# Layer norm's constant as a third entry of the statistics, and a rearranged last token tile, in a Conformer block

## The chip, the cores and the metric

One core of one Trainium2 chip. The metric is the device time of the program in microseconds (us). A profile's span is some 4 us shorter than that time; stages are compared by their place in the span.

Engines: PE is TensorE (matmuls), DVE VectorE, ACT ScalarE, POOL GpSimd, SP SyncE, which issues most transfers.

## The reference, cut to what matters

A Conformer block on tokens `x` of 2 x 4000 x 512 in bf16: feed forward, attention, convolution, feed forward, with a layer norm before each and one at the end.

```python
def _layernorm(x, axis=-1, eps=1e-05):
    m = jnp.mean(x, axis=axis, keepdims=True)
    v = jnp.var(x, axis=axis, keepdims=True)
    return (x - m) / jnp.sqrt(v + eps)
...
h = _layernorm(x3)
h = _silu(h @ w_ff2_a) @ w_ff2_b
x4 = x3 + 0.5 * h
return _layernorm(x4)
```

## The kernel before

Tokens are worked in tiles of 127, four tiles to a chunk. A layer norm is: statistics (`bn_stats`, six values a tile), aggregate (`bn_aggr`, mean and variance), variance plus epsilon, that to the power -1/2 on POOL, normalise. In the head of the kernel and in its last tile each step waits for the one before.

```python
def ln_mean(self, sl, ti):
    self.S.op("DVE", lambda e: e.bn_aggr(self.mv[sl][:, ti, :], self.st[sl][:, ti, :]),
              reads=[self.b_st[sl][ti]], writes=[self.b_mv[sl][ti]])
def ln_factor(self, sl, ti):
    S.op("DVE", lambda e: e.tensor_scalar(self.va[sl][:, ti:ti + 1], self.mv[sl][:, ti, 1:2], EPS, None, ALU.add),
         reads=[self.b_mv[sl][ti]], writes=[self.b_va[sl][ti]])
    S.op("POOL", lambda e: e.tensor_tensor(out=self.rs[sl][:, ti:ti + 1], in0=self.va[sl][:, ti:ti + 1],
                                           in1=self.neghalf[0:TILE, ti:ti + 1], op=ALU.pow),
         reads=[self.b_va[sl][ti], self.b_neghalf], writes=[self.b_rs[sl][ti]])
# ... (ln_aggr does the same for four tiles at once)

def ff_last(self, c, old):                # the last chunk of the kernel
    # ... first matmuls of the feed forward, all 16 blocks
    for ti in range(token_tiles(c)):
        for f in range(FC):                                     # 16 matmuls of 512 columns
            self.ff_second(f, ti, *blocks[f], f == FC - 1)
        self.residual(self.Yb[ti][0:TILE, :], self.b_Y[ti], c * TPC + ti, 0.5)   # XT = XT + 0.5 * Y, on DVE
        self.ln_stats(c, sl, ti)
        self.ln_mean(sl, ti)
        self.ln_factor(sl, ti)
        self.ln_norm(c, sl, ti, self.osb[0][:, ti, :], self.b_osb[0][ti], "DVE")
        self.store_out(c, self.osb[0], self.b_osb[0], ti, ti + 1, ("SP", "ACT"))
```

Waits are placed by a helper. Before each instruction it emits a `wait_ge` for every semaphore value that the engine is not yet known to have seen.

```python
for key in sorted(req, key=str):
    ev = req[key]
    if clk.get(key, 0) >= ev.val:      # this engine has waited for it before
        continue
    if key == e and e in self.NOSELF:  # NOSELF = ("PE",)
        ...
    self.eng[e].wait_ge(self.sem[ev.key], ev.val)
```

## Time and profile before

| what | before |
|---|---|
| time, median of three runs | 2047.35 us (2047.34 to 2047.93) |
| span in the profile | 2043.1 us |
| PE busy | 99% of the span |
| first statistics to PE's fifth block (head) | 7.52 us (3.60 to 11.12) |
| PE's end to the end of the last normalise (tail) | 2.94 us (2037.28 to 2040.22) |
| the last store, from issue to landing | 2.6 us on SP's queue, 2.1 on ACT's |

How to read it: PE runs back to back nearly everywhere, so a step of another engine counts only where PE stands idle for it, and after PE's end. This is the chain of waits of the kernel before in the head (start, length, what; `issue` is time in which the engine waits for nothing that the profile shows):

```profile
4.32 0.19 DVE work L719
4.52 0.02 issue
4.54 0.17 DVE work L724
4.71 0.07 issue
4.78 0.56 POOL work L726
5.34 0.02 issue
5.37 0.16 DVE work L672
5.52 0.10 DVE work L719
```

Each tile goes round aggregate (L719), plus-constant (L724), power (L726), shift (L672), and the next tile's aggregate follows. And this is the kernel before in the transfers' view at the store of the last tile; q14 and q8 are queues that the profile labels "instruction" (packets, MB, share of 16 engines); the last number of an issue is us to landing:

```profile
q14 instruction: 3, 0.02, 2.2%
q10 hardware_dynamic: 30, 0.02, 2.0%
...
out_dram<-work SPq DMA_DIRECT2D x1, 112.0 KB, 2.6
out_dram<-work ACTq DMA_DIRECT2D x1, 15.0 KB, 2.1
```

### The profile page before, as it was taken

Reading aid. Unit: us, or ns where it says so; the run is one execution under the profiler, and the core shown is the slowest. Engines: PE = TensorE matmul, PEld = TensorE weight load, DVE = VectorE, ACT = ScalarE, POOL = GpSimd, SP = SyncE. Lnnn points to the kernel's source line nnn. Section 1 sums busy time; section 2 is a strip of 40 time slices with the busy share of each in tenths; the row PEclk is TensorE's granted clock in tenths of the full one; section 3 lists DMA queues with packets and bytes.
Section 4 is the critical chain, followed back from the end, with each engine's and each line's share of the span. In section 5 each row is a group of like instructions: output and inputs, shape, how many; then the busy total and the mean of one; then the engine's idle time right before and its main releaser. Section 6 shows DMA issues by size and latency. Waiting matters only on the chain.

```text
span 2043.1 us, 24518 instructions
## 1 busy us (share of the span) xinstructions
PE 2029.6 (99%) x9649; PEld 1028.9 (50%) x9649; DVE 1093.0 (54%) x2264; ACT 743.9 (36%) x1274; POOL 109.4 (5%) x236
## 2 busy tenths in 40 slices
PE   9999999999999999999999999999999999999998
PEld 5555555554444444445444444444445555555555
DVE  4244443334556667666766676667674444434434
ACT  3433333333333333333333333333345443443433
POOL 1000000000000000000000000000011000000000
PEclk9999999999999999999999999999999999999999
DMA  8222245320101111114421111111143111111111
GB/s 185 52 62 62 53 101 124 96 70 8 26 16 29 24 31 26 29 24 96 106 55 23 28 29 29 24 28 29 39 135 93 32 31 42 32 31 41 28 35 38
DMA packets 253121, 104.42 MB, mean 51 GB/s; under 512 B 193412, under 2 KB 252487, under 8 KB 252999
## 3 DMA queue, kind: packets, MB, share of 16 engines
q1 hardware_dynamic: 252751, 102.61, 21.1%
q8 instruction: 78, 1.28, 0.3%
q14 instruction: 44, 0.36, 0.1%
q10 hardware_dynamic: 248, 0.18, 0.0%
HBM read 33.77 MB, written 23.34 MB: 28 GB/s over the span
## 4 chain that ended last, share of the span: by engine, by line
PE 97%; DVE 1%; issue 0%; POOL 0%; DMA 0%; ACT 0%; POOLq 0%; SPq 0%; DVEq 0%; ACTq 0%
PE s L500 55%; PE y L500 42%; DVE work L612 0%; DVE wff L1177 0%; POOL work L726 0%; ACT work L550 0%; DVE xt L753 0%; DMA work<-work 0%; DMA xt<-in_x_dram 0%; DVE work L634 0%; POOL work L1186 0%; DVE work L547 0%; DVE wff L1071 0%; DVE work L920 0%; DVE work L719 0%
## 5 line engine op out<-in xcount | busy, mean ns | idle before, releaser
L550 ACT ACTIVATE work<-s 128x508 bf16<-128x508 f32 (+3 forms) x1060 | 621.7, 587 | 1212.8 <-PE s L500 1208.3
L500 PE MATMUL s<-work,wff 128*128 128x508 bf16 (+5 forms) x2624 | 628.2, 371 | 2.3 <-DVE work L547 1.8
L500 PE MATMUL s<-work,keys 128*128 128x508 bf16 (+1 forms) x2048 | 516.7, 374 | 0.1
L500 PE MATMUL y<-work,keys 128*128 128x508 bf16 (+2 forms) x2048 | 504.3, 373 | 0.4 <-DVE work L1000 0.4
L500 PE MATMUL y<-wff,work 128*127 128x512 bf16 x1992 | 501.2, 379 | 0.0
L920 DVE TENSOR_TENSOR work<-work 128x508 f32<-128x508 f32 (+2 forms) x496 | 334.6, 675 | 279.9 <-ACT work L550 278.8
L500 PEld LDWEIGHTS s<-work,wff 128*128 128x128 bf16 x2624 | 252.2, 98 | 278.6 <-issue 6.2
L500 PEld LDWEIGHTS y<-wff,work 128*127 128x127 bf16 x1992 | 273.7, 137 | 171.4
L500 PEld LDWEIGHTS s<-work,keys 128*128 128x128 bf16 x2048 | 199.5, 98 | 231.9 <-issue 0.6
L500 PEld LDWEIGHTS y<-work,keys 128*128 128x128 bf16 (+1 forms) x2048 | 193.5, 97 | 234.0 <-issue 6.2
L753 DVE SCALAR_TENSOR_TENSOR xt<-y,xt 127x512 bf16<-127x512 f32 x126 | 78.5, 683 | 360.1 <-PE y L500 360.1
L612 DVE BATCH_NORM_STATS2 work<-xt 127x6 f32<-127x512 bf16 x312 | 197.3, 680 | 6.3 <-DMA xt<-in_x_dram 6.2
L500 PE MATMUL s<-work 128*127 128x512 bf16 (+3 forms) x776 | 197.0, 378 | 2.2 <-DVE work L1293 1.2
L621 POOL TENSOR_TENSOR work<-work 127x4 f32<-127x4 f32 (+1 forms) x76 | 76.5, 1007 | 1133.0 <-DVE work L619 1133.0
L500 PEld LDWEIGHTS s<-work 128*127 128x127 bf16 (+1 forms) x776 | 94.9, 124 | 76.9 <-issue 3.7
L634 DVE TENSOR_SCALAR work<-xt,work 127x512 bf16<-127x512 bf16 x307 | 110.8, 407 | 26.2 <-POOL work L621 22.9
L753 DVE SCALAR_TENSOR_TENSOR xt<-s,xt 127x512 bf16<-127x512 f32 x55 | 38.0, 692 | 144.6 <-PE s L500 144.6
L753 DVE SCALAR_TENSOR_TENSOR xt<-s,work,xt 127x512 bf16<-127x512 f32 x64 | 48.0, 751 | 32.1 <-PE s L500 31.5
L1075 DVE SCALAR_TENSOR_TENSOR wff<-wff,s 128x508 bf16<-128x508 f32 (+1 forms) x57 | 38.7, 679 | 41.6 <-PE s L500 41.4
L550 ACT ACTIVATE wff<-s 128x508 f32<-128x508 f32 (+1 forms) x67 | 39.5, 591 | 55.1 <-PE s L500 55.1
L550 ACT ACTIVATE work<-keys,work 128x508 bf16<-128x508 bf16 (+1 forms) x68 | 52.3, 775 | 1.4 <-DVE work L1191 1.3
L1156 POOL COPY wff<-wff 128x1 bf16<-128x1 bf16 x56 | 10.4, 187 | 635.3 <-DVE wff L1075 632.8
(83 smaller groups left out, 424.5 us busy)
## 6 DMA issues: line engine op xcount, KB each, us to landing
keys<-keysd SPq DMA_DIRECT2D x62, 128.0 KB, 2.3
keysd<-work SPq DMA_DIRECT2D x14, 448.0 KB, 3.2
out_dram<-work SPq DMA_DIRECT2D x14, 448.0 KB, 3.2
dcvd<-wff SPq DMA_DIRECT2D x48, 127.0 KB, 1.7
keys<-dcvd SPq DMA_DIRECT2D x12, 508.0 KB, 4.9
xt<-in_x_dram SPq DMA_DIRECT2D x13, 448.0 KB, 4.8
wff<-in_w_ff_a_dram SPq DMA_DIRECT2D x16, 256.0 KB, 5.4
work<-work SPq DMA_TRANSPOSE x208, 2.5
```

The lines of the kernel that those rows point to most:

```text
L500: self.S.op("PE", lambda e: e.matmul(out, lhsT, rhs, start=start, stop=stop, **kw), reads=reads, writes=[bank], inc=stop if inc is None el ...
L550: return self.S.op("ACT", lambda e: e.activation(out, in_, func, **kw), reads=reads, writes=writes)
L612: self.S.op("DVE", lambda e: e.bn_stats(self.st[sl][:, ti, :], x), reads=[b_x], writes=[self.b_st[sl][ti]])
L621: S.op("POOL", lambda e: e.tensor_tensor(out=self.rs[sl][:, 0:n], in0=self.va[sl][:, 0:n], in1=self.neghalf[0:TILE, 0:n], op=ALU.pow), rea ...
L634: self.S.op("DVE", lambda e: e.tensor_scalar(out, x, self.mv[sl][:, ti, 0:1], self.rs[sl][:, ti:ti + 1], ALU.subtract, ALU.mult), reads=[b ...
L753: self.S.op("DVE", lambda e: e.scalar_tensor_tensor(out=self.XT[g][rows], in0=ps[rows], scalar=scalar, in1=self.XT[g][rows], op0=ALU.mult, ...
L920: S.op("DVE", lambda e, p=p, n=n, acc=acc: e.tensor_tensor(out=acc, in0=acc, in1=self.P[p][0:n, 0:W], op=ALU.add), reads=[self.b_P[p], sel ...
L1075: self.S.op("DVE", lambda e: e.scalar_tensor_tensor(out=out, in0=th, scalar=1.0, in1=ps[:, 0:W], op0=ALU.add, op1=ALU.mult), reads=[b_ps, ...
L1156: S.op("POOL", lambda e: e.tensor_copy(self.G[gs][:, jj, 0:1], self.G[gp][:, jj, CHUNK:CHUNK + 1]), reads=[self.b_G[gp][jj]], writes=[self ...
```

## The change

First intent: no separate plus-constant. `bn_stats` leaves two entries of three values for a tile. Each tile's statistics get a third entry, set once, of 0, 0 and `D * EPS`, which adds to the sum of squares and to nothing else; the aggregate over nine values instead of six then yields variance plus epsilon by itself.

Second intent, the last tile only: the residual becomes a matmul with twice the identity, so PSUM holds 2·x3 + h, twice x4 (the layer norm does not mind the factor, if epsilon is taken four times: two from the third entries of the two halves, two from the square root's bias); the tile is made in two halves of 256 columns in two PSUM banks, so that the statistics of the first lie beside PE's second; the power on POOL becomes a square root on ACT and a reciprocal on DVE; and DVE and ACT normalise a half each.

```diff
-        self.st = [small(TPC * 6, ...)]
+        self.st = [small(TPC * 9, ...)]
...
 def ln_factor(self, sl, ti):
-        S.op("DVE", lambda e: e.tensor_scalar(self.va..., self.mv[sl][:, ti, 1:2], EPS, None, ALU.add), ...)
-        S.op("POOL", lambda e: e.tensor_tensor(out=self.rs..., in0=self.va[sl][:, ti:ti + 1], ...pow))
+        S.op("POOL", lambda e: e.tensor_tensor(out=self.rs..., in0=self.mv[sl][:, ti, 1:2], ...pow))
...     # the same in ln_aggr
 def ff_last(self, c, old):
+        S.op("DVE", lambda e: e.tensor_scalar(self.two, self.ident, 2.0, None, ALU.mult), ...)
...
+        self.act(self.nr1, self.onef, AF.Sqrt, [self.b_onef], [self.b_nr1])      # loads the table early
-        for ti in range(token_tiles(c)):
+        for ti in range(n - 1):
...
+        halves = [(self.Yb[k], self.b_Y[k], slice(m * D // 2, (m + 1) * D // 2)) for m, k in enumerate((0, ti))]
+        for m, (ps, b_ps, d) in enumerate(halves):
+            self.mm(ps[0:TILE, d], self.two[0:TILE, 0:TILE], self.XT[g][:, d], True, False, ...)
+            for f, (p, b_p) in enumerate(blocks):
+                self.mm(ps[0:TILE, d], p[:, ti * TILE:(ti + 1) * TILE], self.Wb[:, f, d], False, f == FC - 1, ...)
+            S.op("DVE", ... e.bn_stats(st[:, m, 0:6], ps[0:TILE, d]))
+        S.op("DVE", ... e.bn_aggr(self.mv[sl][:, ti, :], st.rearrange("p t s -> p (t s)")))   # 18 values
+        self.act(sd, self.mv[sl][:, ti, 1:2], AF.Sqrt, ..., bias=self.eps2[0:TILE])
+        S.op("DVE", ... e.reciprocal(self.rs[sl][:, ti:ti + 1], sd))
+        S.op("DVE", ... e.scalar_tensor_tensor(out=sh, in0=mean, scalar=-1.0, in1=rs, ...))  # shift
+            # half 0: DVE tensor_scalar (x - mean) * rs;  half 1: ACT Identity, scale=rs, bias=sh
+        self.store_out(c, self.osb[0], b_o, ti, ti + 2, ("SP", "ACT"))
...
 def constants(self):
+        for sl in range(self.LN_SLOTS):
+            S.op("DVE", ... e.memset(self.st[sl][:, :, 6:8], 0.0))
+            S.op("DVE", ... e.memset(self.st[sl][:, :, 8:9], D * EPS))
+        S.op("POOL", ... e.memset(self.eps2, 2 * EPS))
```

More of the change, by code (lines that the diff above doesn't have):

```diff
@@ L384, in memory @@
         self.b_late = [A.buf("late", k * 1024, 2 * CHUNK) for k in range(FC - self.NP)]
+        self.two = A.view(60 * 1024, 128)
+        self.b_two = A.buf("two", 60 * 1024, 256)
         ns = self.LN_SLOTS
@@ L396, in memory @@
         self.b_neghalf = Buf("neghalf")
-        self.st = [small(TPC * 6, parts=TILE).rearrange("p (t s) -> p t s", t=TPC) for _ in range(ns)]
+        self.st = [small(TPC * 9, parts=TILE).rearrange("p (t s) -> p t s", t=TPC) for _ in range(ns)]
         self.b_st = [[Buf("st") for _ in range(TPC)] for _ in range(ns)]
@@ L400, in memory @@
         self.b_mv = [[Buf("mv") for _ in range(TPC)] for _ in range(ns)]
-        self.va = [small(TPC, parts=TILE) for _ in range(ns)]
-        self.b_va = [[Buf("va") for _ in range(TPC)] for _ in range(ns)]
         self.rs = [small(TPC, parts=TILE) for _ in range(ns)]
@@ L412, in memory @@
         self.b_nr1 = Buf("nr1")
+        self.eps2 = small(1)
+        self.b_eps2 = Buf("eps2")
         self.onef = small(1)
@@ L611, in ln_stats @@
         x, b_x = self.tokens(c, ti, src)
-        self.S.op("DVE", lambda e: e.bn_stats(self.st[sl][:, ti, :], x), reads=[b_x], writes=[self.b_st[sl][ti]])
+        self.S.op("DVE", lambda e: e.bn_stats(self.st[sl][:, ti, 0:6], x), reads=[b_x], writes=[self.b_st[sl][ti]])
     def ln_aggr(self, sl, n, shift=False):
@@ L618, in ln_aggr @@
                  reads=[self.b_st[sl][ti]], writes=[self.b_mv[sl][ti]])
-        S.op("DVE", lambda e: e.tensor_scalar(self.va[sl][:, 0:n], self.mv[sl][:, 0:n, 1], EPS, None, ALU.add),
-             reads=self.b_mv[sl], writes=self.b_va[sl])
-        S.op("POOL", lambda e: e.tensor_tensor(out=self.rs[sl][:, 0:n], in0=self.va[sl][:, 0:n],
+        S.op("POOL", lambda e: e.tensor_tensor(out=self.rs[sl][:, 0:n], in0=self.mv[sl][:, 0:n, 1],
                                                in1=self.neghalf[0:TILE, 0:n], op=ALU.pow),
-             reads=self.b_va[sl] + [self.b_neghalf], writes=self.b_rs[sl])
+             reads=self.b_mv[sl] + [self.b_neghalf], writes=self.b_rs[sl])
         if shift:
@@ L723, in ln_factor @@
         S = self.S
-        S.op("DVE", lambda e: e.tensor_scalar(self.va[sl][:, ti:ti + 1], self.mv[sl][:, ti, 1:2], EPS, None, ALU.add),
-             reads=[self.b_mv[sl][ti]], writes=[self.b_va[sl][ti]])
-        S.op("POOL", lambda e: e.tensor_tensor(out=self.rs[sl][:, ti:ti + 1], in0=self.va[sl][:, ti:ti + 1],
+        S.op("POOL", lambda e: e.tensor_tensor(out=self.rs[sl][:, ti:ti + 1], in0=self.mv[sl][:, ti, 1:2],
                                                in1=self.neghalf[0:TILE, ti:ti + 1], op=ALU.pow),
-             reads=[self.b_va[sl][ti], self.b_neghalf], writes=[self.b_rs[sl][ti]])
+             reads=[self.b_mv[sl][ti], self.b_neghalf], writes=[self.b_rs[sl][ti]])
     def store_keys(self, c):
@@ L795, in ff_last @@
         S, late = self.S, FC - self.NP
+        S.op("DVE", lambda e: e.tensor_scalar(self.two, self.ident, 2.0, None, ALU.mult), reads=[self.b_ident], writes=[self.b_two])
         blocks = []
@@ L807, in ff_last @@
             self.tick()
-        sl = self.nxt("ln", self.LN_SLOTS)
-        for ti in range(token_tiles(c)):
+        self.act(self.nr1, self.onef, AF.Sqrt, [self.b_onef], [self.b_nr1])
+        sl, n = self.nxt("ln", self.LN_SLOTS), token_tiles(c)
+        for ti in range(n - 1):
             for f in range(FC):
@@ L817, in ff_last @@
             self.store_out(c, self.osb[0], self.b_osb[0], ti, ti + 1, ("SP", "ACT"))
+        ti, g = n - 1, c * TPC + n - 1
+        st, b_st = self.st[sl][:, ti:ti + 2, :], self.b_st[sl][ti:ti + 2]
+        halves = [(self.Yb[k], self.b_Y[k], slice(m * D // 2, (m + 1) * D // 2)) for m, k in enumerate((0, ti))]
+        for m, (ps, b_ps, d) in enumerate(halves):
+            self.mm(ps[0:TILE, d], self.two[0:TILE, 0:TILE], self.XT[g][:, d], True, False, [self.b_two, self.bx[g]], b_ps)
+            for f, (p, b_p) in enumerate(blocks):
+                self.mm(ps[0:TILE, d], p[:, ti * TILE:(ti + 1) * TILE], self.Wb[:, f, d], False, f == FC - 1,
+                        [self.b_Wb[f], b_p], b_ps)
+            S.op("DVE", lambda e, m=m, ps=ps, d=d: e.bn_stats(st[:, m, 0:6], ps[0:TILE, d]), reads=[b_ps], writes=[b_st[m]])
+        S.op("DVE", lambda e: e.bn_aggr(self.mv[sl][:, ti, :], st.rearrange("p t s -> p (t s)")),
+             reads=b_st, writes=[self.b_mv[sl][ti]])
+        sd, b_sd = self.sh[sl][:, ti:ti + 1], self.b_sh[sl][ti]
+        self.act(sd, self.mv[sl][:, ti, 1:2], AF.Sqrt, [self.b_mv[sl][ti], self.b_eps2], [b_sd], bias=self.eps2[0:TILE])
+        S.op("DVE", lambda e: e.reciprocal(self.rs[sl][:, ti:ti + 1], sd), reads=[b_sd], writes=[self.b_rs[sl][ti]])
+        o, b_o = self.osb[0][:, ti, :], self.b_osb[0]
+        mean, rs, sh = self.mv[sl][:, ti, 0:1], self.rs[sl][:, ti:ti + 1], self.sh[sl][:, ti:ti + 1]
+        b_mv, b_rs, b_sh = self.b_mv[sl][ti], self.b_rs[sl][ti], self.b_sh[sl][ti]
+        S.op("DVE", lambda e: e.scalar_tensor_tensor(out=sh, in0=mean, scalar=-1.0, in1=rs, op0=ALU.mult, op1=ALU.mult),
+             reads=[b_mv, b_rs], writes=[b_sh])
+        for m, (ps, b_ps, d) in enumerate(halves):
+            if m == 0:
+                S.op("DVE", lambda e, ps=ps, d=d: e.tensor_scalar(o[:, d], ps[0:TILE, d], mean, rs, ALU.subtract, ALU.mult),
+                     reads=[b_ps, b_mv, b_rs], writes=[b_o[ti]])
+            else:
+                self.act(o[:, d], ps[0:TILE, d], AF.Identity, [b_ps, b_sh, b_rs], [b_o[ti + 1]], bias=sh, scale=rs)
+        self.store_out(c, self.osb[0], b_o, ti, ti + 2, ("SP", "ACT"))
     def store_out(self, c, o, b_o, lo, hi, engs=("SP",)):
@@ L1293, in constants @@
         S.op("DVE", lambda e: e.memset(self.zero, 0.0), writes=[self.b_zero])
+        for sl in range(self.LN_SLOTS):
+            S.op("DVE", lambda e, sl=sl: e.memset(self.st[sl][:, :, 6:8], 0.0), writes=self.b_st[sl])
+            S.op("DVE", lambda e, sl=sl: e.memset(self.st[sl][:, :, 8:9], D * EPS), writes=self.b_st[sl])
         S.op("POOL", lambda e: e.memset(self.hl, 0.0), writes=self.b_hl)
@@ L1297, in constants @@
         S.op("POOL", lambda e: e.memset(self.onef, 1.0), writes=[self.b_onef])
+        S.op("POOL", lambda e: e.memset(self.eps2, 2 * EPS), writes=[self.b_eps2])
         S.op("DVE", lambda e: e.memset(self.XT[SHARED][HALF - 32:HALF], 0.0), writes=[self.bx[SHARED]])
```

## The prediction

> **What bounds the kernel now.** I read the page first (busy shares, the slices, the chain that ended last), then the waits, then the timeline and the chain of waits in the few stretches where TensorE is not the one that is busy.
>
> ```profile
> span 2043.1 us, 24518 instructions
> PE 2029.6 (99%) x9649; PEld 1028.9 (50%) x9649; DVE 1093.0 (54%) x2264; ACT 743.9 (36%) x1274; POOL 109.4 (5%) x236
> ...
> PE 97%; DVE 1%; issue 0%; POOL 0%; DMA 0%; ACT 0%; POOLq 0%; SPq 0%; DVEq 0%; ACTq 0%
> ...
> L619 DVE TENSOR_SCALAR work<-work 127x4 f32<-127x4 f32 x73 | 12.6, 172 | 2.5
> ```
>
> TensorE (PE) works for 99% of the span and is 97% of the chain that ended last. So of the first part of the change, which takes away one small VectorE (DVE) instruction per layer norm (the group L619 above, and L724 of 15 instructions at 146 ns), almost everything lies beside PE: 12.6 + 2.2 = 14.8 us of DVE work go, but DVE is busy 54% of the time and nobody waits for it. What can move the end are the places where PE stands still and a layer norm is the cause: the head, the last transposes before the convolution, the two chains around 1520 and 1547 us, and the tail. The tail, in the timeline:
>
> ```profile
> 2033.66 1.89 PE L500 MATMUL y<-wff,keys 128*127 128x512 bf16 x8
> ...
> 2035.39 1.89 PE L500 MATMUL y<-wff,work 128*127 128x512 bf16 x8
> ...
> 2036.37 0.41 DVE L634 TENSOR_SCALAR work<-xt,work 127x512 bf16<-127x512 bf16 x1 [0.67 <-POOL work L726]
> 2037.32 0.69 DVE L753 SCALAR_TENSOR_TENSOR xt<-y,xt 127x512 bf16<-127x512 f32 x1 [0.54 <-PE y L500]
> 2038.04 0.69 DVE L612 BATCH_NORM_STATS2 work<-xt 127x6 f32<-127x512 bf16 x1
> 2038.77 0.18 DVE L719 BATCH_NORM_AGGREGATE work<-work 127x2 f32<-127x6 f32 x1
> 2038.99 0.15 DVE L724 TENSOR_SCALAR work<-work 127x1 f32<-127x1 f32 x1
> 2039.22 0.55 POOL L726 TENSOR_TENSOR work<-work 127x1 f32<-127x1 f32 x1 [2.89 <-DVE work L724]
> 2039.81 0.41 DVE L634 TENSOR_SCALAR work<-xt,work 127x512 bf16<-127x512 bf16 x1 [0.66 <-POOL work L726]
> ```
>
> The reader is to see a strictly serial chain: PE ends at 2037.27 (residual's start less a hop of 0.05), then residual, statistics, aggregate, plus-constant, power, normalise, each 0.03 to 0.08 after the one before, until 2040.22. From there to the span's end at 2043.1 are 2.9 us of store (its issue at 2040.29, landing 2.6 us later), which the change leaves as it is: the same two pieces on the same two queues. The part that can shrink is 2.95 us, 0.14% of the kernel.
>
> **What the Trainium skill says.** (1) "TensorE: Matmul & The Clock Gate", Back-to-back issue gap: N/2.4 + 2.5 ns, 262 cycles for 256 columns, so about 109 ns. The trace has 254 columns at 107 ns in the head (20 matmuls, of which 16 with 254 columns, in 2.77 us) and 512 columns at 216 ns (8 in 1.89 us, the last one's own 379 ns counted). It agrees. (2) The same page, Weight-path perf modes: fast weight load needs a full 128-column weight. The tail's weights have 127 columns, and their load row says 137 ns against 98 ns for 128 columns, so they are slower, as stated. This matters, because the halves give each load only 107 ns of matmul to hide behind. (3) "ScalarE: Activation LUTs", What ACT_TABLE_LOAD costs: a table load of 1283 ns (the trace: 1283 exactly, four times) and a fixed cost plus 93 ns per pointer operand of an ACTIVATE (the trace: 604 ns for 127x512 out of PSUM without pointers, 766 with two; agrees within 25 ns). Its next section says that cheap functions such as identity are in every set; the trace has four loads in all, with copies and identities among silu, exp and sigmoid, so the final identity after the square root should bring no load of its own. (4) "PSUM — Partial Sum Buffer", PSUM bank collisions: two engines may not use one bank at a time. The change puts the halves in two banks, so DVE can read the first while PE writes the second. No run yet shows what would happen otherwise.
>
> **The tail, step by step.** Removed after PE's end: residual 0.69, plus-constant 0.15, power 0.55, and half of the statistics; the residual becomes a matmul with twice the identity, and the statistics of half one run while PE makes half two.
> PE: before 16 x 0.216 = 3.45 us, now 2 x 17 = 34 matmuls of 256 columns, 34 x 0.1077 = 3.66. PE ends 0.2 later.
> Half one's PE ends 1.83 after the tile begins (2033.83), at 2035.7. Its statistics wait in DVE's order behind tile 1's normalise (until 2036.78, now 0.2 earlier as tile 1 loses its plus-constant: 2036.6), run to about 2037.0 and are done before PE's end at 2037.47. Hidden.
> Statistics of half two out of PSUM: 674 ns for 512 columns in f32, and 690 against 620 ns for 508 and 444 columns, so 1.09 ns a column; 256 fewer give about 0.41, hop 0.05.
> Aggregate of 18 values: 179 ns for 6, 223 for 15, 250 for 21: about 0.235, hop 0.04.
> Square root on ScalarE (ACT): 202 ns for 128x1, a bias pointer on top: 0.25, hop 0.04.
> Reciprocal: 183 ns for 127x4, so 0.16, hop 0.04. Shift: 0.16 (as L672 in the head), hop 0.04.
> Normalise: ACT's half is last, as it alone needs the shift: 766 - 256 x 0.83 = 0.55, hop 0.04. (0.83 from the page's 593 ns for 508 and 490 ns for 381 columns.) DVE's half, out of PSUM where 512 columns took 806 ns and not 414, is some 0.5 from 0.1 after the shift's start and ends first.
> Sum after PE: 0.46 + 0.275 + 0.29 + 0.20 + 0.20 + 0.59 = 2.02 against 2.95, less the 0.2 that PE takes more: **0.73 us won**.
>
> **The other places.** With the constant in the aggregate, the plus-constant goes, so the power starts about 0.2 us after the aggregate's start instead of 0.4, or much earlier where the plus-constant stood in DVE's queue behind the next tile's statistics. The aggregate itself grows by 3 values, 5 ns each.
>
> The chain of waits around 1550:
>
> ```profile
> 1549.40 0.10 DVE work L719
> 1549.50 0.58 DVE work L612
> 1550.08 0.05 DVE work L724
> 1550.13 0.08 DVE work L672
> 1550.21 0.56 POOL work L726
> 1550.77 0.03 issue
> 1550.80 1.53 DVE work L634 x2
> 1552.33 0.61 DVE xt L547
> 1552.93 0.05 issue
> 1552.98 0.63 PE y L528 x8
> ```
>
> Tile 2's aggregate ends at 1549.50, but its power begins at 1550.21, because L724 waits behind the statistics. Without L724 it begins at 1549.57 and ends at 1550.12; the two normalises begin at 1550.2 and not 1550.8. ACT's copy of the other pair (1552.69, 1.02 long) then becomes nearly the last, so I count 0.45 of the 0.6.
> At 1520 to 1529 the same thing happens, but there ACT's own row of work (1527.46 to 1529.42) ends as late as DVE's: 0.15.
> Before 1498, PE waits 0.35 for four transposes that issue one after another from 1491.76; the power ends 0.1 to 0.2 earlier but DVE is occupied until 1491.24: 0.05.
> The head: each tile's cycle there is 1.1 us (shifts L672 at 5.37, 6.47, 7.57), bound by aggregate, plus-constant, power, shift. It becomes 0.9, so ACT's second normalise, which PE's first blocks wait for, starts 0.4 earlier. But PE's third block needs the second piece of the first weight matrix, issued at 4.44 and landing 3.9 us later at 8.34; it is used at 8.57 now, and would be wanted at 8.17. So the transfer takes the place of the wait: 0.2 counted. The eight new memsets of the statistics' third entry lie on DVE before the first tile arrives; at about 0.1 each (59 ns and a hop) they take 0.8 of the 1.00 us that DVE idles there. Free, narrowly.
> The rest of the new work (table load, twice the identity on DVE, a memset on POOL) falls where those engines idle: ACT has nothing after 2027.45 but store issues until the square root at 2038.2.
> Sum: 0.73 + 0.45 + 0.15 + 0.05 + 0.2 = **1.6 us**, 0.08%. All of it should reach the end, since PE runs back to back between these places.
>
> **Rivals.** (a) The weight loads bound the halves. For: 127 columns load in 137 ns, over the 107 of a matmul. Against: eight matmuls with one column and 127-column weights took 0.74 us at 1515.83, (0.74 - 0.196)/7 = 78 ns each, so loads overlap one another. If each pair took 137, PE would end 34 x 0.03 = 1.0 us later still, and the tail would lose 0.3; the total would be 0.6 us won, 2046.8. (b) ACT reloads a table for the identity, or its store of tile 1 sits before the square root: a reload costs 1.3 us or more on the path; total about 2047. The first is spoken against by the four loads above, the second by an issue time of 0.37 us ending near 2037. (c) Nothing outside the tail reaches PE (other engines or transfers fill every gap): then 0.7 won, 2046.6. (d) Everything reaches it, with 0.4 in the head and 0.4 at 1525: 2.2 won, 2045.1. (e) The memsets overrun and delay the first tile: 0.2 lost.
>
> **Range and chances.** 2047.35 - 1.6 = **2045.7 us**. Rivals (a) to (c) reach up to 2047.0, (d) down to 2045.1, and three runs of before spread by 0.6: **2044.6 to 2047.0** for 8 in 10. The whole stake is 0.1 to 0.15% against the 2% that counts: chances 0.004 faster, 0.99 same, 0.006 slower.
>
> **What would show it.** Right: in the tail 34 matmuls of 256 columns at 107 to 110 ns; first-half statistics wholly before PE's end; from PE's end to the last normalise 2.0 us and not 2.95; five table loads in all, none after the square root; the normalises at 1550 about 0.6 earlier; PE's third block in the head waiting for a transfer. Wrong: a pitch near 137 ns in the tail, a gap on DVE before half two's statistics, a wait of ACT before the square root, the first statistics later than 3.60, or the stretch between 1554 and 2027 longer or shorter than before, which nothing here explains.

## More of the kernel before

The program starts with the loads of the first four token tiles and then, on SP's queue, the pieces of the two weight matrices in turns:

```python
for k in range(self.NWA):
    self.load_wa(i["w_ff1_a"], k, "SP")
    self.load_wb(i["w_ff1_b"], 2 * k, 2 * k + 2)
    if k == 3:
        self.load_x(1)
```

## The result, and the profile after

| | before | after |
|---|---|---|
| median of four runs each, us | 2047.64 (2047.34 to 2047.93) | 2046.24 (2045.57 to 2046.69) |
| span in the profile, us | 2043.1 | 2042.7 |

The ratio is 0.9993, with a 95% interval of 0.9976 to 1.001. Ratios here are the mean time of one kernel's fast runs over that of the other's of the same rounds, so not quite the ratio of the medians. The profiled run of the changed kernel was the slowest of its four (2046.69), which will matter.

The page of the changed kernel shows the small DVE instructions gone, 80 fewer of them net, and PE's busy time unchanged:

```profile
span 2042.7 us, 24546 instructions
## 1 busy us (share of the span) xinstructions
PE 2029.6 (99%) x9665; PEld 1031.0 (50%) x9667; DVE 1081.5 (53%) x2184; ACT 746.2 (37%) x1278; POOL 109.0 (5%) x236
```

The tail, in the timeline (start, length, engine, line, instruction; in brackets idle time before it and what ended that):

```profile
2035.78 1.04 PE L504 MATMUL y<-wff,work 128*127 128x256 bf16 x8
2035.85 0.43 DVE L830 BATCH_NORM_STATS2 work<-y 127x6 f32<-127x256 f32 x1
2036.85 0.43 DVE L830 BATCH_NORM_STATS2 work<-y 127x6 f32<-127x256 f32 x1 [0.57 <-PE y L504]
2037.32 0.24 DVE L831 BATCH_NORM_AGGREGATE work<-work 127x2 f32<-127x18 f32 x1
2037.59 0.29 ACT L554 ACTIVATE work<-work 127x1 f32<-127x1 f32 x1 [9.36 <-DVE work L831]
2037.92 0.16 DVE L835 RECIPROCAL work<-work 127x1 f32<-127x1 f32 x1 [0.36 <-ACT work L554]
2038.11 0.16 DVE L839 SCALAR_TENSOR_TENSOR work<-work 127x1 f32<-127x1 f32 x1
2038.19 0.54 DVE L843 TENSOR_SCALAR work<-y,work 127x256 bf16<-127x256 f32 x1
2038.31 0.56 ACT L554 ACTIVATE work<-y,work 127x256 bf16<-127x256 f32 x1 [0.42 <-DVE work L839]
```

The first half's statistics (2035.85 to 2036.28) are over 0.53 us before PE's end, as planned. The last normalise ends at 2038.87, 1.35 us earlier in the span than before (2040.22). Yet the span is only 0.4 us shorter. The missing 0.95 us is in the one part that the prediction held fixed, the store; in the transfers' view of the changed kernel:

```profile
q8 instruction: 1, 0.02, 3.0%
q14 instruction: 2, 0.02, 2.5%
q10 hardware_dynamic: 28, 0.01, 1.8%
...
out_dram<-work SPq DMA_DIRECT2D x1, 112.0 KB, 3.6
out_dram<-work ACTq DMA_DIRECT2D x1, 15.0 KB, 3.4
```

The same 112 KB take 3.6 us and not 2.6, and a packet of queue q8 appears among them that was not in this window before. (16 KB: one packet, 0.02 MB.)

Where the 1.35 us come from is read by laying the two traces beside each other: the difference between the start of the same instruction in both, at points between which PE runs back to back.

| at | after minus before | gained in the step | predicted |
|---|---|---|---|
| first statistics | +0.23 | -0.23 (first tile landed later) | 0 |
| PE's fifth block (11.1) | +0.12 | 0.11 | 0.2 |
| after the transposes (1498) | -0.08 | 0.20 | 0.05 |
| 1529 | -0.27 | 0.19 | 0.15 |
| 1554 | -0.74 | 0.47 | 0.45 |
| tile 1's residual (2033.9) | -0.74 | 0.00 | 0 |
| end of the last normalise | -1.35 | 0.61 | 0.73 |
| end of the span | -0.40 | -0.95 (store) | 0 |

Two of these places in the chain of waits. Around 1550, where a power had waited behind the next tile's statistics, the changed kernel's two normalises on DVE start at 1549.96 and not at 1550.80, and the chain now runs through ACT's copies, as foreseen:

```profile
1547.09 4.13 ACT work L554 x6
1551.22 0.49 ACT xt L554
1551.71 0.05 issue
1551.76 1.12 PE y L532 x16
```

At 1498, the chain of the kernel before and then of the changed one:

```profile
1495.63 2.48 DMA work<-work
1498.11 0.25 issue
1498.36 0.81 PE s L500 x3
```

```profile
1497.37 0.75 PE y L504 x4
1498.12 0.15 issue
1498.28 0.81 PE s L504 x3
```

Before, PE's chain goes back to a transfer, one of the transposes; after, that has landed in time and PE follows on its own work.

### The profile page after: what moved, and what is told of

Read it like the earlier page. It is cut to its first block, busy times and chain, and to the rows that moved or that the text cites. A ratio compares the mean times of both kernels' runs of the same rounds, so it can differ in the third digit from the quotient of the medians.

```text
span 2042.7 us, 24546 instructions
## 1 busy us (share of the span) xinstructions
PE 2029.6 (99%) x9665; PEld 1031.0 (50%) x9667; DVE 1081.5 (53%) x2184; ACT 746.2 (37%) x1278; POOL 109.0 (5%) x236
## 4 chain that ended last, share of the span: by engine, by line
PE 98%; DVE 1%; ACT 1%; POOL 0%; issue 0%; DMA 0%; SPq 0%; DVEq 0%; ACTq 0%
PE s L504 56%; PE y L504 42%; ACT work L554 0%; DVE wff L1207 0%; DMA xt<-in_x_dram 0%; DVE work L616 0%; POOL work L1216 0%; DVE xt L753 0%; PE y L532 0%; DVE work L551 0%; DVE wff L1101 0%; ACT keys L554 0%; DVE work L674 0%; POOL work L726 0%; DVE work L1214 0%
## 5 line engine op out<-in xcount | busy, mean ns | idle before, releaser
L504 PE MATMUL y<-wff,work 128*127 128x512 bf16 (+1 forms) x2000 | 501.6, 379 | 0.0
```

What stands on the lines that cost most here:

```text
L504: self.S.op("PE", lambda e: e.matmul(out, lhsT, rhs, start=start, stop=stop, **kw), reads=reads, writes=[bank], inc=stop if inc is None el ...
```

## The experiments

Twelve runs were made, in three groups, each group on one chip (the second and third on the same one) with runs of the kernel before among them. Every one computed the right result.

### The kernel before, again

No edit.

> The kernel before, once more, against itself: the floor of what can be told apart. Expected: ratio 1.000, runs within 0.7 us of one another. Its profile: first tile landed at 3.57 us in the first profile, last store 2.6 us from issue to landing. If both move by some tenths here, with no change at all, then what the changed kernel showed there (3.80 us, and 3.6 us) is chance (theory 1); if they come out at 3.57 and 2.6 again, the change is to blame (rival).

Median of five 2047.2 us (2047.12 to 2048.02) against 2047.75 for the nine runs beside it; ratio 0.9999 (0.9985 to 1.0012). In its profile every stage lies 0.10 to 0.13 us behind the first profile of before, a shift already there at the fifth block and constant to the end: the first tile's load landed 0.13 us later. So stage lengths repeat to about 0.02 us, while the landing of the first tile is chance. The store took 2.5 and 2.0 us. The runs spread by 0.9 us, not by the 0.7 expected.

### The changed kernel, again

No edit.

> The changed kernel, once more. Theory 1 (first landing and last store vary by chance): the last normalise ends 1.2 to 1.6 us earlier than in the kernel before, the store lands in 2.3 to 3.6 us, and the time is 1.2 to 1.6 us less than before. Rival (the change makes the store slower by 1 us, or the first landing later by 0.2 us): the store takes 3.4 to 3.7 us again, the first tile lands at 3.8 again, and the time is 0.3 to 0.7 us less than before.

Median 2047.13 us; the five runs were 2046.09, 2046.15, 2047.13, 2047.45 and 2047.55; ratio 0.9997 (0.9984 to 1.0011). The stage gains repeat: 0.22 at 1498, 0.20 at 1529, 0.47 at 1554. The head does not: it took 7.74 us against 7.41, because PE's third block waited 0.23 us for its piece of the weights. The store took 3.1 and 2.9 us in the profiled run, which was the fastest. So the first timing's gain of 1.4 us was more than the kernel gives as a rule; here 0.6 is left. Neither expectation came true whole: the last normalise ended 1.38 us earlier than in the kernel before of this group and the store lay in theory 1's range, but the time won was the rival's.

### The constant alone

The changed kernel with the tail of before:

```diff
-        self.act(self.nr1, self.onef, AF.Sqrt, [self.b_onef], [self.b_nr1])
-        sl, n = self.nxt("ln", self.LN_SLOTS), token_tiles(c)
-        for ti in range(n - 1):
+        sl = self.nxt("ln", self.LN_SLOTS)
+        for ti in range(token_tiles(c)):
...     # the whole block for the last tile is gone
```

> Only the constant as a third entry of the statistics; the tail as before. Theory 1: PE's last stretch begins 0.7 us earlier than before (0.2 by the head, 0.1 to 0.2 before 1498, 0.2 around 1525, 0.45 around 1550), and the tail itself is shorter by 0.2 (one small instruction less in the serial chain): 0.7 to 1.0 us won. Rival (transfers and other engines fill every gap): 0.2 us won, by the tail alone.

Median 2046.46 us (2046.27 to 2046.64); ratio 0.9994 (0.9981 to 1.0008). All five runs lie below all nine of before (lowest 2047.11): of the whole group this was the fastest kernel, though it has only half of the change. 0.7 to 1.0 us were expected; the medians differ by 1.3, the profiled spans by 0.5 (2043.1 to 2042.6), so the medians hold something that the profiles do not show. By stages it won 0.22 + 0.19 + 0.47 us in the three middle places and kept a fast store, 2.6 and 2.1. Its tail won 0.10, not the 0.2 of a whole instruction: from the power's end to the normalise it is now 0.11 us and was 0.04, because the normalise has to wait for two semaphores.

Its head was 0.44 us *longer* than before. PE's timeline in it:

```profile
7.99 0.61 PE L504 MATMUL s<-work,wff 128*128 128x127 bf16 x8 [0.17 <-ACT work L554]
9.06 0.62 PE L504 MATMUL s<-work,wff 128*128 128x127 bf16 x8 [0.46 <-DMA wff<-in_w_ff_a_dram]
```

PE's first two blocks are done and the third waits 0.46 us for the second piece of the weights, issued at 4.44 and landed 4.6 us later, at 9.0.

### The tail alone

The kernel before with the new last tile, entries of six values, and epsilon all in the square root's bias:

```diff
+            S.op("DVE", lambda e, m=m, ps=ps, d=d: e.bn_stats(st[:, m, :], ps[0:TILE, d]), ...)
...     # the rest of the last tile as in the change
+        S.op("POOL", lambda e: e.memset(self.eps2, 4 * EPS), writes=[self.b_eps2])
```

> Only the new last token tile; every layer norm elsewhere as before. Theory 1: PE's last stretch begins when it did before (within 0.1 us), the last normalise ends 0.6 us earlier than before: PE 0.27 later, then 2.07 us instead of 2.95. 0.6 us won, and together with the constant's part the two add up to the whole change. Rival: the store is slower by 1 us when two engines release it, and the time is 0.3 us more than before.

Median 2047.35 us (2046.95 to 2047.84) against 2047.75; ratio 0.9999 (0.9985 to 1.0013). The stages before the tail lie a constant 0.23 to 0.25 us behind, as they should with nothing changed in them (its first tile landed at 3.84). The tail ended 0.6 us earlier by itself, and 0.2 of that was given back in the store, which took 2.7 and 2.9 us. So by stages the two parts are independent, and the middle gains belong wholly to the constant. The medians of this group do not add up: 1.3 for the constant and 0.4 for the tail, against 0.6 for both, as head and store came out differently.

### Without the halves

One pass of 17 matmuls of 512 columns; DVE normalises alone:

```diff
-        for m, (ps, b_ps, d) in enumerate(halves):
-            ...
+        self.mm(ps[0:TILE, :], self.two[0:TILE, 0:TILE], self.XT[g], True, False, ...)
+        for f, (p, b_p) in enumerate(blocks):
+            self.mm(ps[0:TILE, :], p[:, ti * TILE:(ti + 1) * TILE], self.Wb[:, f, :], False, f == FC - 1, ...)
+        S.op("DVE", lambda e: e.bn_stats(self.st[sl][:, ti, 0:6], ps[0:TILE, :]), ...)
+        self.ln_mean(sl, ti)
...
+        S.op("POOL", lambda e: e.memset(self.eps2, 3 * EPS), writes=[self.b_eps2])
```

> The last tile as one pass of 17 matmuls with 512 columns; residual on PE and square root on ScalarE stay, VectorE normalises alone. Arithmetic: PE 17 x 0.216 = 3.67 (as with halves); after PE: statistics 0.67 and not 0.43, aggregate 0.20, square root 0.29, reciprocal 0.16, normalise 0.81 with no shift before it, hops 0.25: 2.4 us from PE's end, against 2.07 with halves and 2.95 before. The store: theory S (in the changed tail a 16 KB packet of the instruction queue falls into the store's packets, because TensorE's instructions are half as long each and its prefetch comes later): here PE's matmuls are 512 columns again, so the instruction packet falls as before, between the stores, and the last store lands in 2.4 to 2.7 us. Rival (the new residual, square root or store time itself slow it): 2.9 us or more on both queues again.

A single run, here and in the next three. From PE's end to the last normalise 2.34 us, 0.28 more than the 2.06 with halves. The halves' extra matmul costs little: 34 of 256 columns last 3.72 us in the changed kernel, 17 of 512 at 216 ns each make 3.67. So the two halves, together with two engines normalising, are worth about 0.23 us. The store was fast, 2.3 and 2.1. The whole took 2046.9 us against 2047.37, with a long head (8.42 us, third block waiting 0.91 for its weights).

### One engine normalises

```diff
-        S.op("DVE", lambda e: e.scalar_tensor_tensor(out=sh, in0=mean, scalar=-1.0, in1=rs, ...))
         for m, (ps, b_ps, d) in enumerate(halves):
-            if m == 0:
+            if True:
```

> As changed, but VectorE normalises both halves, one after the other, and no shift is made. The two normalises are 0.54 each and overlap by little: from the reciprocal's end 0.04 + 1.0 to 1.1, against 0.04 + 0.16 + 0.04 + 0.56 = 0.80 with two engines: 2.3 us from PE's end instead of 2.07. Store: theory S says slow again (2.9 to 3.6 us), as PE is untouched; the rival that the release by two engines slows the store says 2.4 to 2.7.

From PE's end to the last normalise 2.30 us, 0.24 more than with two engines: DVE's two halves take 0.99 us where shift and ACT's half had taken 0.76 (2038.11 to 2038.87). The expectation of a slow store was missed: it took 2.4 and 2.6 us. The whole, 2045.66 us against 2047.37, was the best of this group although its tail is longer, because its head (7.32, no wait for weights) and its store were both good. This is what made the store the chief question.

### The power on POOL

```diff
-        self.act(self.nr1, self.onef, AF.Sqrt, [self.b_onef], [self.b_nr1])
+        S.op("DVE", ... e.memset(self.st[sl][:, n - 1:n + 1, 8:9], 2 * D * EPS))
...
-        self.act(sd, self.mv[sl][:, ti, 1:2], AF.Sqrt, ..., bias=self.eps2[0:TILE])
-        S.op("DVE", lambda e: e.reciprocal(self.rs[sl][:, ti:ti + 1], sd), ...)
+        self.ln_factor(sl, ti)
```

> As changed, but the power on GpSimd in place of square root and reciprocal. From the aggregate's end to the shift: hop 0.07 + 0.56 + hop 0.03 to 0.10 = 0.7, against 0.02 + 0.30 + 0.03 + 0.17 + 0.02 = 0.54 measured: 0.15 to 0.2 us slower, 2.25 us from PE's end. It also has no table load for the square root (four loads, not five). Store: theory S says slow again (2.9 to 3.6).

2.23 us from PE's end to the last normalise, 0.17 more than with ACT's square root (0.29) and the reciprocal (0.16), since the power alone takes 0.55. The store took 3.1 and 3.3 us, so neither the square root nor its table has to do with the slow store. The whole took 2047.07 us against 2047.37, with a long head (8.44 us, third block waiting 0.94 for its weights).

### Sixteen dummy matmuls after the last tile

What is q8? Over the program it moved 78 packets of 16 KB, and PE has 19,298 matmuls and loads (9,649 of each), 247 to a packet. The Trainium skill, "Runtime: NRT & Kernel Launch", section Instruction fetch mechanics, states that engines fetch their instructions in blocks of 16 KiB, 256 instructions each, over a DMA queue of their own, and calls the cost mostly hidden. The traces agree: in the kernel before, PE starts 256 instructions, as the median, from one of q8's packets to the next, and no other engine has even 3,000 in all. If q8 carries PE's instructions, more work for PE after the last tile should move q8's last packet away from the store; if the slow store came from two engines releasing it, or from its closeness to tile 1's store, it should stay slow.

```diff
+        for k in range(16):
+            self.mm(self.Sb[0][0:TILE, 0:D // 2], self.two[0:TILE, 0:TILE], self.XT[g][:, 0:D // 2], True, True,
+                    [self.b_two, self.bx[g]], self.b_S[0], inc=k == 15)
         S.op("DVE", lambda e: e.bn_aggr(self.mv[sl][:, ti, :], st.rearrange("p t s -> p (t s)")), ...)
```

Nothing waits for these matmuls; they write a bank that is free.

> As changed, with 16 matmuls of 256 columns more on TensorE behind the last real one, into a bank that nobody reads (the result stays right). They take 1.75 us on PE beside the chain. Theory S: the instruction queue's 16 KB packets come about 1.7 us later, the last of them after the store's packets: the store lands in 2.4 to 2.8 us on both queues. Rival: 2.9 to 3.6 as before. The span may still end later if PE's own end then is last.

The dummies in PE's timeline, then the transfers' view of the same kernel at the store:

```profile
2037.67 1.91 PE L504 MATMUL s<-xt,keys 127*127 127x256 bf16 x16
```

```profile
q10 hardware_dynamic: 30, 0.02, 2.2%
q14 instruction: 2, 0.02, 2.1%
...
out_dram<-work SPq DMA_DIRECT2D x1, 112.0 KB, 2.4
out_dram<-work ACTq DMA_DIRECT2D x1, 15.0 KB, 2.2
```

q8's packet is gone from the store's window and the store is fast again. Still two engines release it, and the normalise of tile 1 still starts 1.33 us before the last statistics (1.32 without dummies): those two rivals fall. The whole run was 2046.73 us against 2047.37, because its head was the longest of all, 8.53 us with a wait of 0.80 for weights; that comes long before the dummies.

The raw transfer records give the size of it. Start of q8's last 16 KB packet, counted from the store's first packet, with that packet's own duration; and the store's landing on SP's and on ACT's queue, all in us:

```
kernel         q8's last starts   lasts    store lands after (SP, ACT)
before_again        -2.83         1.14         2.5  2.0
before              -2.51         0.95         2.6  2.1
const_only          -2.50         1.25         2.6  2.1
before_third        -2.24         0.96         2.5  2.0
no_halves           -1.74         1.01         2.3  2.1
one_norm            -0.49         0.95         2.4  2.6
repeat              -0.34         1.30         3.1  2.9
tail_only           -0.28         1.07         2.7  2.9
after               +0.09         1.30         3.6  3.4
head_order          +0.11         1.58         3.7  3.9
pool_pow            +0.12         0.95         3.1  3.3
repeat2             +0.25         1.27         3.5  3.3
best                +1.68         1.05         2.3  2.5
pe_dummies          +2.09         0.98         2.4  2.2
```

Where the packet starts within about a third of a us of the store's first packet, on either side, the store is slow; where it is over by then, or begins when the store's last packet has gone (0.96 in the best kernel), it is fast. The store's 127 packets of 1 KB take 46 ns each as a rule; a few early ones took over 100 in every kernel. What differs is the end. In the changed kernel the last eight packets straggle, starting 1.37 to 2.07 us after the first, five of them with 116 to 174 ns; in the kernel before the last eight start at 0.58 to 0.66 and take 46 each. Eight of 127 is the share of one of the 16 transfer engines, so the picture is of one engine held by the 16 KB packet; the records do not name the engine. In one_norm 0.46 us of overlap remained and cost some 0.5 on ACT's queue: counted from PE's end, the store had begun 0.24 us later than in the changed kernel, behind the longer normalise, and the packet had come 0.34 us earlier, by no edit of its own.

### A third profile of before, the changed kernel again, and the weights' order

The first two are without edit. The third issues the second weight piece earlier:

```diff
+        self.load_wa(i["w_ff1_a"], 0, "SP")
+        self.load_wa(i["w_ff1_a"], 1, "SP")
         for k in range(self.NWA):
-            self.load_wa(i["w_ff1_a"], k, "SP")
+            if k > 1:
+                self.load_wa(i["w_ff1_a"], k, "SP")
             self.load_wb(i["w_ff1_b"], 2 * k, 2 * k + 2)
```

> The kernel before, for its head on this chip: where does the second piece of the first weight matrix land? In three profiles with the head as before it took 3.4, 3.8 and 3.9 us from its issue; in seven with the constant in the statistics 3.9, 4.2, 4.3, 4.6, 4.9, 5.1 and 5.2. Theory W (it varies from chip to chip and run to run, and the change only removed the slack of 0.2 us that hid it): here it may come anywhere from 3.4 to 5.2, and then the old head waits for it too. Rival (the change makes it slower): below 4.0 again, while the changed kernel of the same call shows over 4.1.

2047.08 us in one look; head 7.52 us from 3.71 us on, store 2.5 and 2.0: the same as the other profiles of before. The piece landed 3.7 us after its issue, and 4.1 in the changed kernel of the same group: that is in line with the rival (below 4.0, and over 4.1 in the changed kernel, met only at its edge). Theory W allowed 3.4 to 5.2, so one landing does not refute it.

> The changed kernel a third time, beside the ones that mend it. First statistics to the fifth matmul block (the first with 254 columns): 7.4 to 8.3 us, with a wait for the weights in TensorE's third block. Store 2.9 to 3.6 us. 0.6 to 1.4 us won against before.

Median 2046.93 us (2046.56 to 2047.39) against 2047.22 (eight runs, 2047.07 to 2047.62); ratio 0.9999 (0.9985 to 1.0013). Head 7.39 us, with no wait to speak of in the third block, against the expectation; store 3.5 and 3.3. 0.3 us won, less than the 0.6 to 1.4 expected.

> As changed, but the second piece of the first weight matrix is issued before the first piece of the second one, 0.5 us earlier. If the head's wait is for that piece's turn in a full transfer queue, it lands about 1 us earlier and TensorE's third block follows the second without a gap: 7.3 us from the first statistics to the fifth block (as in the one run in which nothing was waited for), 0.1 to 0.9 us less than the changed kernel of this call; 1.4 to 1.9 us less than before. If something else of the head has become the bound, the gap stays.

Median 2046.56 us (2046.08 to 2046.72); ratio 0.9995 (0.9981 to 1.001). The piece is issued at 3.89 instead of 4.44, lands in 3.3 to 3.4 us, and no block waits for it. The head did not get shorter for all that: 7.53 us, as the warm-up matmuls ran later than in other runs (five of them took 2.16 us instead of 1.6) and the first transposes began at 6.95 instead of 6.44. One kernel with the old order shows the same (the dummies, 2.32), and the next one, with the new order, does not (1.59), so the order does not seem to be the cause. The store was the slowest of all, 3.7 and 3.9.

### Both mends together

The weights' order and the dummy matmuls, on the changed kernel.

> Both mends: the weight's piece earlier, and 16 unread matmuls behind the last real one, that move TensorE's instruction packets out of the store. Head as in the run with the order alone; store 2.2 to 2.5 us, 0.5 to 1.0 less than the changed kernel's; so 0.5 to 1 us less than the order alone, and about 2.2 to 2.6 us less than the kernel before.

Median 2045.49 us (2045.16 to 2045.59) against 2047.22 of before and 2046.93 of the changed kernel in the same rounds; ratio to before 0.999 (0.9976 to 1.0005). The interval includes 1, but the five runs lie below every run of both others: 1.7 us less than before, 1.4 less than the change as it was. Against the weights' order alone it is 1.1 us less, and no run of one overlaps the other: that is the dummies, and in the profiled runs 0.2 of it the warm-up's chance in the other's head. The 2.2 to 2.6 us expected against before were too many. Head 7.33 us, store 2.3 and 2.5. In its chain of waits, the head:

```profile
4.36 0.21 DVE work L721
4.56 0.07 issue
4.64 0.56 POOL work L726
5.20 0.03 issue
5.23 0.02 DVEq L152
5.25 0.06 issue
5.31 0.16 DVE work L674
```

The plus-constant is out of the circle, but between the power (L726) and the shift (L674) there is now a wait instruction of DVE's own queue (L152) and 0.06 us after it, which the circle of before did not have.

## Why the prediction was right or wrong

The predicted 2045.7 us was right within the range by the first timing (2046.24), and the direction by the medians of all three timings of the unedited change (0.3 to 1.4 us below before; its fourteen runs lie between 2045.57 and 2047.55). But its sum of 1.6 us came near partly by luck: the first timing's medians differ by 1.4, the two profiled spans by 0.4, and the later timings by 0.6 and 0.3. Three terms were confirmed, two were mis-sized, and one that stood at nought was the largest.

**The store: the step that failed.** The prediction said of the time from the last normalise to the end: "2.9 us of store ... which the change leaves as it is: the same two pieces on the same two queues." The pieces and queues are the same, and in the changed kernel's four profiles with an unedited tail (three of the change, one with the weights' order) the store took 0.5 to 1.1 us longer on SP's queue. A 16 KB packet of q8, by its count the queue of PE's instructions, falls into it. That the packet is what slows the store is shown: fourteen profiles order themselves by its place, and moving it by 2 us with work that nothing waits for brought the store back. What brings the two together is seen in part: q8's last packet follows the end of PE's work. It starts 1.0 to 1.6 us after PE's end in the five profiles whose last tile has 512 columns, and 2.6 to 3.3 us after it in the nine with halves (with dummies, after the end of the dummies), while the store comes 0.9 us sooner after PE's end. In all of them it starts 3.1 to 3.9 us after the packet before it, which starts when PE has 13 to 19 instructions left in the first case and at most 5 in the second. Sixteen dummies of 1.9 us moved the last packet by 2.0 us against the store, and in the best kernel by 1.6. Why the last packets come when they do stays open: that PE's queue fetches some way ahead, through matmuls now half as long, is only argued.

**The middle.** 0.45 was counted at 1550, 0.47 measured, and the place of the wait moved to ACT's copies as said. 0.15 at 1520 to 1529, 0.19 to 0.20 measured. At 1498 the step was "DVE is occupied until 1491.24: 0.05"; measured 0.20 to 0.22. The mistake was to take DVE's queue as fixed: the removed instruction stood in that same queue, so everything behind it moved up, and so did the four transposes; PE's gap went from 0.35 to 0.15 us, and what is left is its own issue.

**The head.** The step "It becomes 0.9" failed by one term: the circle is 1.0 us (shifts at 5.51, 6.51 and 7.51). The plus-constant had also been the instruction that waited for the aggregate on DVE's behalf. With it gone, the shift must wait for that as well as for POOL, and the helper emits a wait instruction for it: from the power's end to the shift it is now 0.10 to 0.12 us and was 0.03, so 0.07 to 0.08 more a circle. That the transfer of the second weight piece would take the place of the wait was right in kind; its size is the other miss. The prediction took the 3.9 us landing as given. It was 3.4 to 3.9 us in the four heads of before but 3.9 to 5.2 in the eight heads with the constant and the old order, and PE's third block waited up to 0.94 us for it. So 0.2 won were counted, and it was 0.2 won at best and 1.0 lost at worst. Both kinds of head have moved about the same bytes by 7 us, some 1.2 MB. Why the piece lands later with the constant stays open. All eight landings with it are as late as the latest of the four without, or later; by chance alone such an order would come about once in 250 times (4 of 12, one tie), so that the change itself delays the piece is the likelier reading. No run shows how. Issuing the piece earlier took the wait away in both profiles that did so, whatever the cause.

**The tail.** From PE's end on 2.02 us were predicted and 2.06 measured, term by term: statistics of a half 0.43 (0.41), aggregate 0.24 (0.235), square root 0.29 (0.25), reciprocal and shift 0.16 each (0.16), ACT's half 0.56 (0.55). PE took 0.27 longer, not 0.2: 109.4 ns a matmul instead of 107.7, so 3.72 us for 34 and not 3.66. The trace of before already had it: the 254-column matmuls of the head start 109 ns apart, not the 107 that the prediction read. Two other readings were off without effect: the last tile's first matmul starts at 2033.66, not 2033.83, and the two ACT rows give 0.81 ns a column, not 0.83. The gain is 0.61 to 0.64, not 0.73. The parts by experiment: square root on ACT 0.17, second engine 0.24, halves with that second engine 0.23.

**The rivals.** (a), weight loads bounding the halves at 137 ns: refuted by the 109.4. (b), a reload of a table: refuted; five loads in all, the last at 2026.73, right after the last silu, and the identity brings none (nor does the store of tile 1 delay the square root, which starts 0.03 us after the aggregate):

```profile
2026.73 1.28 ACT L554 ACT_TABLE_LOAD   x1
```

(c), only the tail reaches the end: refuted by the constant alone, which won 0.88 us in the middle. (d), 0.4 in the head and 0.4 at 1525: neither came. (e), the memsets delaying the first tile: DVE ends them 0.3 to 0.6 us before the tile lands, and the tile landed as late (3.73 and 3.84) in two kernels that have no such memsets; free, as said. So one of the prediction's signs of being wrong, first statistics later than 3.60, came true (3.83) without the memsets as its cause.

So the sum, for the first pair of profiles: 0.86 in the middle, 0.11 in the head less 0.23 of chance, 0.61 in the tail, which makes 1.35; less 0.95 in the store, 0.40. For the best kernel the store's loss is gone, and the span is 1.8 us shorter than before (2041.3 against 2043.1).

What stays open beside the landing of the weight piece: the repeated change gave two runs near 2046.1 and three near 2047.3. Head and store both varied by enough for that, but only the profiled run of the five could be read. The kernel before does the same: of its nine runs in that group four lie at 2047.11 to 2047.30 and five at 2047.75 to 2048.00, and its three profiled runs (2046.86, 2047.20 and 2047.08) are all of the faster kind. So part of what the medians show as gain may lie where no trace was taken.

## What to carry to other kernels

After removing a step, ask what that step also did: here it had done a wait for the next consumer, and stood in a queue in which everything then moved up. At a scale of a microsecond the end of a kernel is not "a store of fixed length": look whether instruction fetches or other traffic share its transfer engines, and whether the change moves one onto the other. And when a change of several parts gives less than the sum, time the parts alone and read each stage's offset between traces: it told in one table what no timing could.

## What the Trainium skill lacked or had wrong

- "Runtime: NRT & Kernel Launch", Instruction fetch mechanics, calls the fetch mostly hidden. It was hidden from the engines here, but not from a store: with a 16 KB fetch that starts within about a third of a us of its first packet the last store took 2.7 to 3.7 us on SP's queue and not 2.3 to 2.6. "DMA: Bandwidth & Descriptors", Queues, rings and completion order, has each transfer engine take turns between its queues packet by packet, and names a queue for refills, but gives no such cost.
- "TensorE: Matmul & The Clock Gate", Back-to-back issue gap, gives a sustained pace of about 131 ns for 512 columns and 81 for 128, and calls N/2.4 + 2.5 the isolated gap. Sustained streams with a weight load each ran at 216 ns for 512 columns and 109 for 256 and 254: it is the second formula that holds.
- The same page gives a weight load as the column count over 1.2, 106 ns for 127 columns. Here a load's own record is 137 ns, yet pairs of such a load and a one-column matmul ran 78 ns apart, and loads hid wholly behind 109 ns matmuls: the formula is neither the length nor the pace.
- No page that I found gives the aggregate's cost by its number of values: 179, 194, 208, 223, 237 and 250 ns for 6, 9, 12, 15, 18 and 21.
- No page that I found gives the cost of one more wait instruction on DVE ahead of a dependent one: 0.07 to 0.08 us here, half of the 0.15 us of the instruction whose removal caused it.
